# A depth of two for a stretch of input transfers in a fused DeltaNet and gated-MLP kernel

## The chip, the cores and the metric

The kernel runs on one core of one Trainium2 chip. The metric is the device time of one execution in microseconds (us). The runs of the kernel before lie at 631.19, 631.37 and 634.57 us; their median is 631.37 us.

## What is computed

```
for t in range(S):                              # _attn_ref, per batch and head
    y[:, :, t] = einsum('bhd,bhde->bhe', q[:, :, t], state)
    v_old = einsum('bhde,bhd->bhe', state, kt)  # kt: k over its norm
    state = state + bt * einsum('bhd,bhe->bhde', kt, vt - v_old)
...
gate = 1.0 / (1.0 + exp(-(x @ w_gate)))         # _moe_ref, x = y of all heads
val = x @ w_val
return (gate * val) @ w_out
```

There are 4 batches, 8 heads, 768 tokens, and a head dimension of 48. The attention output is seen as 3072 tokens of 384 features; the MLP has 1536 hidden features. All inputs and the output are float32.

## The kernel before

The 768 tokens are cut into 12 groups of 64. For each group the recurrence is solved in blocks: products of keys (`gram`, L298), a small triangular solve on VectorE (DVE) (`solve`, or `solve_halves` for the first three groups), updates of the state (`updates`, `advance`), and the rows of y (`rows`, L509). Then the group's 256 tokens (64 in each of 4 batches) pass through the MLP in 12 hidden tiles of 128: `gate_val` makes the gate and value products on TensorE (PE), L585 for group 0 and L588 later; `gated` takes the sigmoid on ScalarE (ACT), L593, and the product with the value on DVE, L594; `outp` multiplies by the output weights, L613 and L619. The gate products of two tiles alternate between two PSUM buffers, so a tile needs the product L594 of the tile two before it.

The order of the work is written out by hand; each engine executes its instructions in that order. A prologue in straight lines sets up the group 0 recurrence. From the first gate tile on, a loop over slots (`slot`, two for each hidden tile) takes the work of `plan`, `late` and `tail` for the slot, so that pieces of the next groups' recurrence and of the weight preparation stand between the MLP products.

The weights come as 36 pieces of 384 KB, numbered in the order of their use (gate, value and output weights of the hidden tiles, mixed). Each is loaded by `load_piece` (L177) as raw 64-bit words. `scaled(n)` runs two ACT instructions on piece n (L194, L196), and `join` (DVE, L208) makes the float32 weights of it. Pieces 0 to 13 are loaded by `stage` in the prologue. From piece 14 on, `scaled(n)` issues the load of piece n + 6 after its own second instruction (`EAGER, BEHIND = 14, 6`).

All input loads are issued from SyncE (SP), in the order of the program: the weight pieces, the keys (`load_k`, two halves of 192 KB, L110), the queries (`load_q`, two halves of 256 KB, L114), and the rows of keys and values (`load_rows`, 384 KB, L122, with a small load of beta, L125). An issue that has to wait holds all issues behind it on SP. The helper `pace(ins, after)` makes an instruction wait for another one; it is used to hold a load until the DVE or ACT instruction given has ended. The last part of the prologue, where the change lies, contains these loads in this order: pieces 10 and 11 and the queries of group 1, all after `state[0]["joint"]` (DVE, L437); pieces 12 and 13 after `lower_left(1)` (ACT, L370); the first part of the rows of group 1; the keys of group 2; and pieces 14 to 18, one in each `scaled(8)` to `scaled(12)`.

Around and behind these loads stand, in the prediction's steps, `advance(0)` (L531 on ACT), the solve of group 1 with its transposition L429 on DVE and its products `pz` and `pm` (L416) on PE, and the solve's last subtraction L437.

Of the kernel before, what the change touches and what calls it, by code (L numbers as in the profile page):

```python
# [23 lines left out]
B, H, S, D = 4, 8, 768, 48  # L24
# [7 lines left out]
CP = 2 * J  # L32
# [28 lines left out]
def deltanet_gated_mlp(ctx: ExitStack, tc: tile.TileContext, kd, qd, kv, beta, words, out):  # L61
    nc = tc.nc
# [12 lines left out]
    kqp = [const.tile([128, 6, J, C], F32, name=f"kqp{i}") for i in range(2)]  # L75
# [15 lines left out]
    def pace(ins, after):  # L91
        if after is not None:
            tc.add_manual_dep(ins.ins, after.ins.name, mybir.DependencyInfo(mybir.DependencyClass.Sync, mybir.DependencyReason.DATA), reason="pace")
# [7 lines left out]
    def busy_array(out, n, after=()):  # L101

        for i in range(n):
            ins = nc.tensor.matmul(out=out.rearrange("q a b -> q (a b)"), lhsT=flat[:, 0:128], rhs=flat, start=True, stop=True)
            if i < len(after):
                pace(ins, after[i])

    def load_k(g):
        for e in range(2):
            nc.sync.dma_start(kqp[g % 2][64 * e:64 * e + D, 0:2].rearrange("p s c t -> p (s c t)"), kd[g, e])  # L110

    def load_q(g, after=None):
        for e in range(2):
            ins = nc.sync.dma_start(kqp[g % 2][64 * e:64 * e + 64, 2 + 2 * e:4 + 2 * e].rearrange("p s c t -> p (s c t)"), qd[g, e])  # L114
            pace(ins, after)

    def load_rows(g, part):

        st = state[g]
        if "kv" not in st:  # L120
            st["kv"] = wk.tile([128, 2, CP, D], F32, name=f"kv_{g}", tag="kv", bufs=2)
        nc.sync.dma_start(st["kv"][:, part].rearrange("p c d -> p (c d)"), kv[g, :, part * CP * D:(part + 1) * CP * D])  # L122
        if part:
            st["beta"] = wk.tile([128, 32], F32, name=f"beta_{g}", tag="beta", bufs=2)
            nc.sync.dma_start(st["beta"], beta[:, g])  # L125

    def load_group(g):
        load_k(g)
        load_q(g)
        load_rows(g, 1)  # L130
        load_rows(g, 0)
# [42 lines left out]
    def load_piece(n, after=None):  # L174
        f, w = pieces[n]
        raw[n] = wt.tile([128, PW, 2], U32, name=f"raw_{n}", tag=f"w{n}")
        ins = nc.sync.dma_start(raw[n].rearrange("p c w -> p (c w)"), words[3 * f + "gvo".index(w)])  # L177
        pace(ins, after)

    def stage(lo, hi, after=None):  # L180
        for n in range(lo, hi):
            load_piece(n, after)
# [6 lines left out]
    def scaled(n):  # L189

        half, lo, hi = words_of(n)
        nc.scalar.activation(lo.bitcast(I32), half, AF.Copy, bias=-4095.5 / 8192, scale=1 / 8192)  # L194
        h = hi.bitcast(F32)
        done[n] = nc.scalar.activation(h, h, AF.Prelu, scale=2.0 ** -112, alpha=-2.0 ** 32)  # L196
        if n + BEHIND in range(EAGER, len(pieces)):
            load_piece(n + BEHIND, done[n])
# [336 lines left out]
    def flip(g, c):  # L535

        st = state[g]
        if c == 0:
            xx = wk.tile([128, 2, KC, GT], F32R if g else F32, name=f"xx_{g}", tag=f"xx{(g + 1) % 2}", bufs=1)
            st["xh"], st["xl"] = (xx[:, i] for i in range(2))  # L540
        xh, xl, ys = st["xh"], st["xl"], st["ys"][:, c].rearrange("p h e d -> p (h e d)")
        pt = ps_aux.tile([128, KC, 128], F32, name=f"pt_{g}_{c}", tag="aux")
        for k in range(KC):
            nc.tensor.transpose(pt[:, k], ys[:, k * 128:(k + 1) * 128], ident)
        ts = slice(c * 128, (c + 1) * 128)
        if g == 0:
            (nc.vector.tensor_copy if c else nc.scalar.copy)(out=xh[:, :, ts], in_=pt)  # L547
            return
        nc.scalar.copy(xh[:, :, ts], pt)
        nc.vector.tensor_tensor(out=xl[:, :, ts], in0=pt, in1=xh[:, :, ts].bitcast(F32), op=ALU.subtract)  # L550
# [103 lines left out]
    def take(gen, n=1):  # L654
        for _ in range(n):
            next(gen, None)
# [11 lines left out]
    EN = mybir.EngineType  # L668
    ctx.enter_context(tc.manual_schedule(engines={EN.DVE, EN.PE, EN.Activation, EN.Pool, EN.SP}))
    load_k(0)  # L670
    load_rows(0, 1)
    load_q(0)
    stage(0, 3)
    load_k(1)
    stage(3, 6)
    load_rows(0, 0)
# [20 lines left out]
        scaled(n)  # L697
    take(norms1, 11)
    take(halves0, 2)
    stage(10, 12, state[0]["joint"])  # L700
    load_q(1, state[0]["joint"])
    clear(1)
    take(masks0, 2)
# [22 lines left out]
    flip(0, 0)  # L726
    flip(0, 1)
    busy_array(gap[0], 2)
    tail = collections.defaultdict(list)
    for n, at in enumerate((0, 0, 1, 2, 3, 5, 6, 8, 9, 10, 10, 11, 11, 12, 12, 13, 14, 15, 16, 16, 17, 18, 18), 13):  # L730
        plan[at].append(lambda n=n: scaled(n))
# [153 lines left out]
```

## Time and profile before

| | |
|---|---|
| median of 3 runs | 631.37 us (631.19 to 634.57) |
| profiled execution, its own time | 631.45 us |
| span of the profiled execution | 629.7 us |
| PE busy | 610.1 us, 97% of the span |
| DVE busy | 478.4 us, 76% |
| ACT busy | 345.1 us, 55% |
| PE clock granted | 1.00 |
| hardware DMA queue q1 | 17664 packets, 39.53 MB |
| weight pieces | 36 issues of 384 KB, median 6.0 us to landing |

The span runs from the first to the last instruction of the program; the execution's own time has what lies around it too. All times in the profile are counted from the span's start. A timeline row gives start, length, engine, line, operation, what is written and read, the count of merged instructions, and in brackets the idle time of the engine before it and what ended it. A row of a DMA issue gives the count, the size and the median time from the issue to the landing. Names such as L177 are line numbers of the kernel before. SPq rows are issues of transfers by SP. The chain that ended last is followed back from the last instruction, each step to what released it.

### The profile page before, as it was taken

To read this page: it belongs to the slowest core of one execution; us is meant where nothing else is said; L and a number is where in the kernel's file an instruction comes from. 1 tells how busy PE (TensorE), PEld (TensorE's weight loads), DVE (VectorE), ACT (ScalarE), POOL (GpSimd) and SP (SyncE) were. 2 spreads that over 40 slices of the span, in tenths; PEclk is the share of its full clock that TensorE was granted. 3 is DMA by queue.
4 is the path that set the end of the run, shared out by engine and by line. 5 is a ranking of instruction groups with operands and counts; after the bars stand their busy time and mean duration, and the time that the engine had idled before them with its cause. 6 is when DMAs were issued, how large, how long until landed. Compare 5 with 4: busy or idle time off the path is not lost.

```text
span 629.7 us, 25087 instructions
## 1 busy us (share of the span) xinstructions
PE 610.1 (97%) x10990; PEld 566.3 (90%) x10998; DVE 478.4 (76%) x1443; ACT 345.1 (55%) x933; POOL 40.7 (6%) x102
## 2 busy tenths in 40 slices
PE   6789999999999999999999999999999999999996
PEld 3467778899999999999999999999999999999996
DVE  5887887688978978978977977977977977963221
ACT  4889775477446446456456456456456456435222
POOL 6000000000002002002001002002002002001000
PEclk9999999999999999999999999999999999999999
DMA  8495742203113113113113103112113100100101
GB/s 260 179 303 186 248 108 70 55 2 87 28 27 87 27 28 87 28 28 86 28 29 87 27 28 88 26 29 86 28 29 86 26 4 4 26 4 2 26 1 25
DMA packets 17773, 41.13 MB, mean 65 GB/s; under 512 B 4224, under 2 KB 7296, under 8 KB 17664
## 3 DMA queue, kind: packets, MB, share of 16 engines
q1 hardware_dynamic: 17664, 39.53, 22.5%
q8 instruction: 86, 1.41, 0.9%
q14 instruction: 23, 0.19, 0.1%
HBM read 34.80 MB, written 4.72 MB: 63 GB/s over the span
## 4 chain that ended last, share of the span: by engine, by line
PE 89%; DVE 7%; issue 1%; ACT 1%; DMA 1%; ACTq 0%; SPq 0%; DVEq 0%
PE gv L588 44%; PE po L619 21%; PE gv L585 5%; PE pu L488 3%; PE po L613 3%; PE yy L509 2%; PE pg L298 2%; PE pp L326 2%; PE pk L457 2%; PE pd L527 1%; PE pk L480 1%; DVE w L224 1%; PE pm L416 1%; DMA kqp<-in_kd_dram 1%; DVE hg L402 1%
## 5 line engine op out<-in xcount | busy, mean ns | idle before, releaser
L588 PE MATMUL gv<-xx,w 128*128 128x256 f32 x2376 | 311.6, 285 | 0.3 <-DVE xx L550 0.3
L588 PEld LDWEIGHTS gv<-xx,w 128*128 128x128 f32 x2376 | 299.0, 191 | 4.0 <-DVE xx L550 0.6
L619 PE MATMUL po<-w,h 128*128 128x384 f32 x792 | 162.7, 341 | 0.0
L619 PEld LDWEIGHTS po<-w,h 128*128 128x128 f32 x792 | 133.7, 188 | 1.2
L599 ACT CAST h<-sg 128x256 fp32r<-128x256 f32 x132 | 53.5, 405 | 116.0 <-DVE sg L594 115.7
L593 ACT ACTIVATE sg<-gv 128x256 f32<-128x256 f32 x144 | 54.9, 381 | 110.8 <-PE gv L588 103.4
L594 DVE TENSOR_TENSOR sg<-sg,gv 128x256 f32<-128x256 f32 x144 | 60.1, 417 | 66.2 <-ACT sg L593 65.9
L354 DVE TENSOR_TENSOR tmp<-X,gp 128x126 f32<-128x126 f32 (+22 forms) x279 | 73.4, 263 | 8.2
L357 DVE TENSOR_TENSOR X<-X,tmp 128x126 f32<-128x126 f32 (+22 forms) x279 | 72.3, 259 | 8.3
L604 DVE TENSOR_TENSOR h<-sg,h 128x256 fp32r<-128x256 f32 x132 | 54.9, 416 | 12.5 <-ACT h L599 12.4
L564 POOL COPY x<-yt 32x192 f32<-32x192 f32 x72 | 29.4, 409 | 444.6 <-DVE yt L559 441.9
L491 ACT COPY su<-pu 32x384 f32<-32x384 f32 x92 | 43.3, 470 | 10.9 <-PE pu L488 9.1
L284 ACT ACTIVATE kv<-kv,mq 128x48 f32<-128x48 f32 x192 | 47.9, 325 | 0.0
L331 DVE TENSOR_TENSOR kqp<-pp,pmask 64x512 f32<-64x512 f32 x48 | 33.0, 688 | 1.5 <-PE pp L326 0.2
L585 PE MATMUL gv<-xx,u 128*128 128x256 f32 x144 | 33.6, 384 | 0.3 <-DVE xx L547 0.3
L585 PEld LDWEIGHTS gv<-xx,u 128*128 128x128 f32 x144 | 26.7, 190 | 5.1 <-ACT xx L547 0.8
L468 DVE TENSOR_TENSOR R<-kv,pk 128x384 f32<-128x384 f32 x44 | 22.4, 550 | 10.1 <-PE pk L480 9.3
L310 ACT COPY G<-pg 32x256 f32<-32x256 f32 (+1 forms) x69 | 25.4, 368 | 8.0 <-PE pg L298 6.6
L564 ACT COPY x<-yt 32x192 f32<-32x192 f32 x72 | 25.1, 349 | 1.2
L559 DVE STREAM_TRANSPOSE yt<-ys 128x768 f32<-128x768 f32 x9 | 8.8, 979 | 19.9 <-ACT ys L515 19.9
L217 ACT CAST w<-u 128x384 fp32r<-128x384 f32 x36 | 18.0, 507 | 9.3 <-DVE w L224 9.2
L533 DVE TENSOR_TENSOR su<-su,pd 48x384 f32<-48x384 f32 x40 | 22.0, 550 | 0.5
(107 smaller groups left out, 543.6 us busy)
## 6 DMA issues: line engine op xcount, KB each, us to landing
raw<-in_words_dram SPq DMA_DIRECT2D x36, 384.0 KB, 6.0
kv<-in_kv_dram SPq DMA_DIRECT2D x24, 384.0 KB, 3.8
kqp<-in_qd_dram SPq DMA_DIRECT2D x24, 256.0 KB, 4.3
kqp<-in_kd_dram SPq DMA_DIRECT2D x24, 192.0 KB, 3.5
out_dram<-ot SPq DMA_DIRECT2D x48, 96.0 KB, 2.2
beta<-in_beta_dram SPq DMA_DIRECT2D x12, 16.0 KB, 3.5
```

The costliest lines, as they stand in the source:

```text
L284: nc.scalar.activation(V[:, c], V[:, c], AF.Copy, scale=mq[:, c, 0:1])
L354: nc.vector.tensor_tensor(out=tmp, in0=X[:, k:16, j:j + 1].to_broadcast([128, n, j]), in1=gp[:, j:j + 1, 0:j].to_broadcast([128, n, j]), o ...
L357: nc.vector.tensor_tensor(out=X[:, k:16, 0:j], in0=X[:, k:16, 0:j], in1=tmp, op=ALU.add)
L491: (nc.vector.tensor_copy if g == 0 and x else nc.scalar.copy)(out=su[r:r + 32, 2 * x + e], in_=pu[x][r:r + 32])
L564: copy(x[32 * q:32 * q + 32, :, :, a].rearrange("q k c s -> q c k s"), yt[32 * a:32 * a + 32, :, q::4])
L585: nc.tensor.matmul(out=pg[:, o], lhsT=parts[w, f][:, k * 128:(k + 1) * 128], rhs=x[0][:, k], start=k == 0, stop=k == KC - 1)
L588: nc.tensor.matmul(out=pg[:, o], lhsT=parts[w, f][:, a, k * 128:(k + 1) * 128], rhs=x[b][:, k], start=(k == 0 and q == 0), stop=(k == KC - ...
L593: nc.scalar.activation(h, st["gv", f][:, 0], AF.Sigmoid)
L594: nc.vector.tensor_tensor(out=h, in0=h, in1=st["gv", f][:, 1], op=ALU.mult)
L599: nc.scalar.copy(hh[:, 0], st["sg", f])
L604: nc.vector.tensor_tensor(out=hh[:, 1], in0=st["sg", f], in1=hh[:, 0].bitcast(F32), op=ALU.subtract)
L619: nc.tensor.matmul(out=po[s], lhsT=hh[:, a, ts], rhs=parts["o", f][:, w], start=(f == 0 and q == 0), stop=(f == NF - 1 and q == 2))
```

## The change

Every load of keys, queries, rows and weight pieces is noted in a list `sent` as it is issued (the loads of beta are not). While a depth stands in `behind`, each noted load waits, besides what it waited for already, until the load that many positions before it in the list has landed. The depth is 2; it is set just before pieces 10 and 11 are issued, the eleventh and twelfth, and taken away just before the first slot, in which the first gate tile is.

```
+    sent, behind = [], []
+
+    def in_turn(ins):
+
+        if behind and len(sent) >= behind[0]:
+            pace(ins, sent[-behind[0]])
+        sent.append(ins)
+
     def load_k(g):
         for e in range(2):
-            nc.sync.dma_start(...)
+            in_turn(nc.sync.dma_start(...))
...
     def load_q(g, after=None):
...
             pace(ins, after)
+            in_turn(ins)
...
     def load_rows(g, part):
...
-        nc.sync.dma_start(st["kv"][:, part]...)
+        in_turn(nc.sync.dma_start(st["kv"][:, part]...))
...
     def load_piece(n, after=None):
...
         pace(ins, after)
+        in_turn(ins)
...
     take(halves0, 2)
+    behind.append(2)
     stage(10, 12, state[0]["joint"])
     load_q(1, state[0]["joint"])
...
     busy_array(gap[0], 2)
+    behind.clear()
     tail = collections.defaultdict(list)
```

More of the change, by code (lines that the diff above doesn't have):

```diff
@@ L106, in busy_array, with in_turn @@
                 pace(ins, after[i])
+    sent, behind = [], []
+    def in_turn(ins):
+        if behind and len(sent) >= behind[0]:
+            pace(ins, sent[-behind[0]])
+        sent.append(ins)
     def load_k(g):
         for e in range(2):
-            nc.sync.dma_start(kqp[g % 2][64 * e:64 * e + D, 0:2].rearrange("p s c t -> p (s c t)"), kd[g, e])
+            in_turn(nc.sync.dma_start(kqp[g % 2][64 * e:64 * e + D, 0:2].rearrange("p s c t -> p (s c t)"), kd[g, e]))
     def load_q(g, after=None):
@@ L115, in load_q @@
             pace(ins, after)
+            in_turn(ins)
     def load_rows(g, part):
@@ L121, in load_rows @@
             st["kv"] = wk.tile([128, 2, CP, D], F32, name=f"kv_{g}", tag="kv", bufs=2)
-        nc.sync.dma_start(st["kv"][:, part].rearrange("p c d -> p (c d)"), kv[g, :, part * CP * D:(part + 1) * CP * D])
+        in_turn(nc.sync.dma_start(st["kv"][:, part].rearrange("p c d -> p (c d)"), kv[g, :, part * CP * D:(part + 1) * CP * D]))
         if part:
@@ L178, in load_piece @@
         pace(ins, after)
+        in_turn(ins)
     def stage(lo, hi, after=None):
@@ L699, in deltanet_gated_mlp @@
     take(halves0, 2)
+    behind.append(2)
     stage(10, 12, state[0]["joint"])
@@ L728, in deltanet_gated_mlp @@
     busy_array(gap[0], 2)
+    behind.clear()
     tail = collections.defaultdict(list)
```

## The prediction

> **What bounds the kernel now.** I read the page first, then the chain of work that ended last, then the timelines of SP, ACT, DVE and PE one by one over 28 to 72 us, where the changed transfers lie.
>
> ```profile
> span 629.7 us, 25087 instructions
> PE 89%; DVE 7%; issue 1%; ACT 1%; DMA 1%; ACTq 0%; SPq 0%; DVEq 0%
> ...
> 42.45 5.42 PE L585 MATMUL gv<-xx,u 128*128 128x256 f32 x24 [0.31 <-DVE xx L547]
> 47.80 1.16 PE L298 MATMUL pg<-kqp 48*64 48x64 f32 x64
> ```
>
> The whole kernel is a PE stream: 89% of the chain is PE. From the first gate tile at 42.45 us (the rows with start, length, engine, line and what is written) PE is fed almost without a break, so whatever stops it there for a moment is added to the end. Loads matter only where they make somebody late for PE. These are the loads concerned, on SP's queue (start, length of the issues, line, count), and the DVE instruction that releases the first:
>
> ```profile
> 28.27 0.69 DVE L437 TENSOR_TENSOR mt<-mt,pm 128x512 f32<-128x512 f32 x1 [0.44 <-PE pm L416]
> ...
> 28.98 1.29 SPq L177 DMA_DIRECT2D raw<-in_words_dram  x2
> 30.32 1.11 SPq L114 DMA_DIRECT2D kqp<-in_qd_dram  x2
> 33.22 0.81 SPq L177 DMA_DIRECT2D raw<-in_words_dram  x2
> 34.08 1.27 SPq L122 DMA_DIRECT2D kv<-in_kv_dram  x1
> 35.45 0.88 SPq L110 DMA_DIRECT2D kqp<-in_kd_dram  x2
> 36.42 11.41 SPq L177 DMA_DIRECT2D raw<-in_words_dram  x9
> ```
>
> In program order these are pieces 10, 11, both halves of q(1), pieces 12, 13, rows kv(1) part 0, both halves of k(2), then pieces 14, 15, 16, 17, 18 as their scaling slots come. That is fourteen paced transfers; the last four raw issues of the last row (19 and on) are not paced. Up to eight are in flight at a time, they crowd each other, and each takes long:
>
> ```profile
> raw<-in_words_dram SPq DMA_DIRECT2D x9, 384.0 KB, 6.0
> kqp<-in_kd_dram SPq DMA_DIRECT2D x2, 192.0 KB, 7.0
> ```
>
> (transfers issued from 28.9 to 43 us: count, size, median us from issue to landing). What ACT does with the pieces, one pair L194/L196 for each, piece 12 first:
>
> ```profile
> 40.88 0.56 ACT L194 ACTIVATE raw<-raw 128x384 int32<-128x384 uint16 x1
> 42.14 0.56 ACT L194 ACTIVATE raw<-raw 128x384 int32<-128x384 uint16 x1
> 43.98 0.55 ACT L194 ACTIVATE raw<-raw 128x384 int32<-128x384 uint16 x1 [0.84 <-DMA raw<-in_words_dram]
> 45.59 0.56 ACT L194 ACTIVATE raw<-raw 128x384 int32<-128x384 uint16 x1
> 48.19 0.56 ACT L194 ACTIVATE raw<-raw 128x384 int32<-128x384 uint16 x1
> 48.65 0.56 ACT L196 ACTIVATE raw<-raw 128x384 f32<-128x384 f32 x1
> 49.74 1.93 ACT L531 COPY su<-pd 48x384 f32<-48x384 f32 x4 [0.53 <-PE pd L527]
> 59.52 0.38 ACT L593 ACTIVATE sg<-gv 128x256 f32<-128x256 f32 x1
> ```
>
> The L194 rows are pieces 12, 13, 14, 15 and 17. Only piece 14 is waited for, for 0.84 us; so there is no margin for piece 14 already before the change, and little for the next ones. From 49.74 to 59.52 ACT has no idle time that could take up a delay (next row: stretch, its length, then busy us of PE, PEld, DVE, ACT: 5.85 of 6.00).
>
> ```profile
> 54.00:60.00 6.00, 6.00 (x27) 4.75 (x26) 2.88 (x10) 5.85 (x18) 0.53 (x1) 1.00 0.38 97
> 60.00:66.00 6.00, 5.29 (x282) 4.03 (x281) 5.86 (x15) 4.77 (x16) 0.00 (x0) 1.00 0.64 205
> ```
>
> **The change part by part.** Nothing is removed. It adds bookkeeping at build time, which costs nothing on the chip, and one more wait before each of the fourteen issues. SP executes its queue in order, so each wait also holds everything behind it on SP, and at most two of the fourteen are in flight. Of the fourteen, the first two wait for pieces 8 and 9, which landed long before (SP had stood idle until L437 ended at 28.96), so they keep their start. After that two chains run side by side, each transfer starting when the one two ahead has landed:
> even: piece 10, q(1) first half, piece 12, kv(1), k(2) second half, piece 15, piece 17;
> odd: piece 11, q(1) second half, piece 13, k(2) first half, piece 14, piece 16, piece 18.
>
> The restart after a landing I take as 0.05 us: SP started 0.02 us after L437 ended, and a second wait instruction may stand between. The price of a transfer with one other beside it is the term that decides. It was not run in this form, so it is bounded by rows from quieter stretches:
>
> ```profile
> raw<-in_words_dram SPq DMA_DIRECT2D x1, 384.0 KB, 3.1
> raw<-in_words_dram SPq DMA_DIRECT2D x5, 384.0 KB, 3.5
> raw<-in_words_dram SPq DMA_DIRECT2D x1, 384.0 KB, 3.7
> kv<-in_kv_dram SPq DMA_DIRECT2D x1, 384.0 KB, 3.2
> kv<-in_kv_dram SPq DMA_DIRECT2D x1, 384.0 KB, 3.9
> kqp<-in_qd_dram SPq DMA_DIRECT2D x1, 256.0 KB, 3.6
> kqp<-in_qd_dram SPq DMA_DIRECT2D x1, 256.0 KB, 4.5
> kqp<-in_kd_dram SPq DMA_DIRECT2D x1, 192.0 KB, 2.9
> kqp<-in_kd_dram SPq DMA_DIRECT2D x16, 192.0 KB, 3.3
> ```
>
> The 3.1 is piece 10 itself (issued at 28.98), the 3.5 the median of the five pieces issued from 63 to 72 us, with one or two in flight, the 3.7 a piece issued just behind another, at 67.8 us. The others are from the later loads of a group, which come two to four close together; 3.3 is the median of all later k loads. I take 3.4 for a piece (nearest to the 63 to 72 us stretch, a little less because its last one had three beside it), 3.4 for kv, 3.1 for k, and 3.7 for q (near its low end: its rows are of two halves issued close together, the paced ones will start at the landings of pieces 10 and 11, about 1 us apart).
>
> Even chain: piece 10 lands at 28.98 + 3.1 = 32.1. Then 3.7 + 3.4 + 3.4 + 3.1 + 3.4 + 3.4 = 20.4, with six restarts 0.3, is 20.7: piece 17 lands at 52.8. Low ends: 3.6 + 3.1 + 3.2 + 2.9 + 3.1 + 3.1 + 0.3 = 19.3, at 51.4. High ends: 4.5 + 3.7 + 3.9 + 3.3 + 3.7 + 3.7 + 0.3 = 23.1, at 55.2.
> On the way piece 12 lands at 39.3 (high 40.4), needed at 40.88; k(2) at 45.9 (high 47.7), needed by PE's L298 at 47.80; piece 15 at 49.3 instead of in time for 45.59.
> Odd chain: piece 11 goes 0.4 us behind piece 10 and lands, as the second of a pair (3.7), at 33.1. Piece 13 lands at 40.3 (high 41.4), needed at 42.14: no cost. Piece 14: 3.7 + 3.4 + 3.1 + 3.4 + 0.2 = 13.8, at 46.9 instead of 43.98.
>
> So ACT stands three times: for piece 14 until 46.9, for piece 15 until 49.3, and for piece 17 until 52.8. The waits don't add; each piece is due at an absolute time and the last one decides. The pair for piece 17 takes 48.65 + 0.56 - 48.19 = 1.02 us, so L531, which began at 49.74, begins at about 53.85: ACT is 4.1 us late. It stays 4.1 late to the sigmoid of 59.52 (63.6), as it has no gap between.
>
> Behind that sigmoid stands DVE, and behind DVE stands PE:
>
> ```profile
> 59.93 0.42 DVE L594 TENSOR_TENSOR sg<-sg,gv 128x256 f32<-128x256 f32 x1 [2.94 <-ACT sg L593]
> 66.09 0.70 DVE L429 STREAM_TRANSPOSE scratch<-mt 128x512 f32<-128x512 f32 x1
> 65.24 2.86 PE L585 MATMUL gv<-xx,u 128*128 128x256 f32 x12
> 68.03 0.72 PE L416 MATMUL pm<-scratch 32*32 32x32 f32 x60
> 69.06 0.79 PE L416 MATMUL pm<-scratch 32*32 32x32 f32 x68 [0.31 <-issue]
> ```
>
> DVE's L594 waits for exactly this sigmoid and from it DVE is full (5.86 of 6.00 us from 60 to 66), so L429, which ended at 66.79, ends at 70.9. The products pm read what L429 writes; PE came to them at 68.1 (65.24 + 2.86), 1.3 us after L429, and so could hide 1.3 of the 4.1 us. Now it comes to them at 68.1 and starts at 70.95: 2.85 us lost. Smaller stops of PE before that, for a gate buffer that the late sigmoid frees, are swallowed by this wait. Some 0.2 us may come back, as the 0.31 us in which PE waited for nothing the profile shows, in the middle of pm, can pass while it waits anyway. After pm PE goes on in its order with the delay, and DVE and ACT, later still by up to 1.3 us, have idle time to come back to it:
>
> ```profile
> 74.38 0.42 DVE L594 TENSOR_TENSOR sg<-sg,gv 128x256 f32<-128x256 f32 x1 [1.22 <-ACT sg L593]
> ```
>
> Nothing later is tied to an absolute time, so the rest moves as a block: +2.65 us.
>
> The profiled execution took 631.45 us (its span 629.7 and 1.75 around it), 0.08 over the median 631.37. 631.45 + 2.65 = 634.1. Low prices: L531 at 52.45, 2.7 late, minus 1.3 and 0.3, is +1.1, 632.6. High prices: L531 at 56.25, 6.5 late, minus 1.3, is +5.2, 636.7.
>
> **The rivals.** About 0.5%, 3.16 us here, is what a measurement of this kernel can tell from no change.
>
> *The chain is dearer (slower).* If piece 17 lands after about 53.3, 0.5 us later than I take, the loss passes 3.16 us. That is 0.08 us more per transfer, and q alone at its high end gives 0.8. For it: the high rows above, and that an issue itself took up to 1.27 us (kv at 34.08). Against: with two in flight most crowding is gone. With the middle of its stretch at 54.2 L531 is at 55.25, 5.5 late, the loss 4.1: 635.5.
>
> *The waits are hidden (no change).* If piece 17 lands by 50.0, L531 is at most 1.3 us late and the slack before pm takes it. That needs 17.9 us for six transfers, 2.93 each with the restart; only the lowest k row is that short. Time 631.4.
> [...]
>
> *Not slower, a shade faster.* PE waits twice for nothing that the profile shows while the crowd is in flight:
>
> ```profile
> 31.18 0.28 PE L488 MATMUL pu<-kv,mt 32*32 32x48 f32 x5 [1.31 <-issue]
> 36.56 0.37 PE L488 MATMUL pu<-kv,mt 32*32 32x48 f32 x14 [0.67 <-issue]
> ```
>
> Both lie on the chain before the first gate tile. If the crowd of loads causes the second (the first begins before anything paced differs), a thinner one takes up to 0.67 us away and PE starts the gates earlier. It counts only if piece 17 is in time too, by 50.0; else ACT, which waits for landings, sets the pace anyhow. Time 630.8.
>
> *The change doesn't do what it says.* If the added edge between two issues of one queue made no wait, nothing would change, 631.4. Against it: a wait of the same kind, pace on the instruction given, held SP until 28.98 here.
>
> **How the numbers follow.** Forecast as summed, landing of piece 17 between 50.8 and 53.3 (632.3 to 634.6): 0.50. Dearer chain: 0.38. Hidden: 0.07. Shade faster: 0.03. No wait made: 0.02. Over 0.5% slower is the dearer chain, 0.38; over 0.5% faster only by a cause I don't see, 0.02, taken from the rest; within 0.5% all else, 0.60. The range reaches from just under the low sum into the hidden case, 632.0, to 636.5 near the high sum, leaving 1 in 10 on each side.
>
> **What would show it.** SP's raw issues of the stretch spread from 28.98 to about 50, each soon after a landing, with 3.1 to 3.7 us to landing instead of 6.0; ACT's waits on raw landings rise from 0.84 to some 6 us (3.8 for piece 14, over 1 each for 15 and 17); L531 starts near 53.8; PE shows a wait of 2 to 3 us on DVE's L429 before pm, and later the same idle times as now. It is wrong if piece 17 lands before 50, if PE stops at another place first for longer, or if the delay shrinks again after 75 us.

## The result and the profile after

The changed kernel took 635.83 us (median of 6 runs, 632.97 to 636.26) against 631.08 us (6 runs) before: a ratio of 1.006, 95% interval 1.0032 to 1.0088 (the two medians alone would give 1.0075). It is slower by a little over half a per cent. The execution that was profiled was the quickest of the six, 632.97 us with a span of 631.3, so its trace shows only 1.5 us of the loss; a second profile of the same kernel, further down, shows the rest.

Transfers issued from 28.5 to 49 us in the changed kernel (count, size, median us to landing):

```profile
raw<-in_words_dram SPq DMA_DIRECT2D x7, 384.0 KB, 3.6
kqp<-in_qd_dram SPq DMA_DIRECT2D x2, 256.0 KB, 3.4
kv<-in_kv_dram SPq DMA_DIRECT2D x1, 384.0 KB, 3.2
kqp<-in_kd_dram SPq DMA_DIRECT2D x2, 192.0 KB, 3.1
```

SP's timeline of the same kernel (start, length, what is issued):

```profile
28.61 0.95 SPq L186 DMA_DIRECT2D raw<-in_words_dram  x2
31.78 1.68 SPq L122 DMA_DIRECT2D kqp<-in_qd_dram  x2
35.30 1.18 SPq L186 DMA_DIRECT2D raw<-in_words_dram  x2
```

The median transfer takes 3.1 to 3.6 us, where it took 6.0 (pieces) and 7.0 (keys) before, but each one starts only when the one two ahead of it has landed, so that they come in pairs. ACT's timeline (in brackets the idle time and what ended it; L204/L206 are L194/L196 of before, L541 is L531, L603 is the sigmoid):

```profile
48.18 0.55 ACT L204 ACTIVATE raw<-raw 128x384 int32<-128x384 uint16 x1 [6.43 <-DMA raw<-in_words_dram]
51.10 0.57 ACT L204 ACTIVATE raw<-raw 128x384 int32<-128x384 uint16 x1 [0.79 <-DMA raw<-in_words_dram]
52.81 0.56 ACT L204 ACTIVATE raw<-raw 128x384 int32<-128x384 uint16 x1 [0.41 <-DMA raw<-in_words_dram]
53.71 0.45 ACT L541 COPY su<-pd 48x384 f32<-48x384 f32 x1
```

Those are the waits for pieces 14, 16 and 17. What DVE makes of it, from its timeline:

```profile
63.92 0.42 DVE L604 TENSOR_TENSOR sg<-sg,gv 128x256 f32<-128x256 f32 x1 [2.98 <-ACT sg L603]
70.09 0.70 DVE L439 STREAM_TRANSPOSE scratch<-mt 128x512 f32<-128x512 f32 x1
```

And PE:

```profile
49.94 1.35 PE L595 MATMUL gv<-xx,u 128*128 128x256 f32 x5 [1.31 <-DVE sg L604]
70.94 1.28 PE L426 MATMUL pm<-scratch 32*32 32x32 f32 x128 [2.27 <-DVE scratch L439]
73.54 2.75 PE L595 MATMUL gv<-xx,u 128*128 128x256 f32 x12
```

PE stops twice, 1.31 us before gate tile 2 and 2.27 us before pm. The chain of work that ended last now runs through the loads themselves, one behind the other, up to the late scaling (start, length, what):

```profile
29.04 3.68 DMA raw<-in_words_dram
32.78 3.35 DMA kqp<-in_qd_dram
36.14 3.62 DMA raw<-in_words_dram
39.82 3.20 DMA kqp<-in_kd_dram
43.08 5.07 DMA raw<-in_words_dram
...
49.19 3.59 DMA raw<-in_words_dram
...
70.09 0.71 DVE scratch L439
```

The first five DMA rows are the odd chain of the prediction, from piece 11 to piece 14; the last is piece 17 of the even chain, issued when piece 15 had landed.

### The profile page after: what moved, and what is told of

It is laid out like the page before. It is cut to its first block, busy times and chain, and to the rows that moved or that the text cites. A ratio compares the mean times of both kernels' runs of the same rounds, so it can differ in the third digit from the quotient of the medians.

```text
span 631.3 us, 25085 instructions
## 1 busy us (share of the span) xinstructions
PE 610.0 (97%) x10990; PEld 565.9 (90%) x10998; DVE 478.4 (76%) x1443; ACT 344.7 (55%) x933; POOL 40.7 (6%) x102
## 4 chain that ended last, share of the span: by engine, by line
PE 84%; DVE 7%; DMA 4%; ACT 3%; issue 1%; SPq 0%; ACTq 0%; DVEq 0%
PE gv L598 44%; PE po L629 21%; PE gv L595 3%; PE pu L498 3%; DMA raw<-in_words_dram 3%; PE yy L519 2%; PE po L623 2%; PE pg L308 2%; PE pp L336 2%; PE pk L467 1%; PE pk L490 1%; PE pd L537 1%; DMA kqp<-in_kd_dram 1%; DVE w L234 1%; ACT kv L294 1%
## 5 line engine op out<-in xcount | busy, mean ns | idle before, releaser
L609 ACT CAST h<-sg 128x256 fp32r<-128x256 f32 x132 | 53.5, 405 | 116.2 <-DVE sg L604 115.8
L603 ACT ACTIVATE sg<-gv 128x256 f32<-128x256 f32 x144 | 54.9, 381 | 109.6 <-PE gv L598 103.0
L204 ACT ACTIVATE raw<-raw 128x384 int32<-128x384 uint16 x36 | 20.2, 561 | 8.0 <-DMA raw<-in_words_dram 7.9
```

Of the source, the lines that this page charges most:

```text
L603: nc.scalar.activation(h, st["gv", f][:, 0], AF.Sigmoid)
L609: nc.scalar.copy(hh[:, 0], st["sg", f])
```

## The experiments

Each was timed on the same chip as the kernel before, side by side with it. That kernel's median was 631.17 on the first chip (r1 to r4), 631.60 on the second (r5 to r8) and 632.91 on the third (r9 to r12); so ratios are compared, not times across chips. Theory A is the prediction's: due times, piece 17 and the transposition before pm. B is the PE clock, C a cost of every wait, D a delay that moves on to the next place.

| run | median us | ratio, 95% interval |
|---|---|---|
| r1 changed kernel again | 636.24 | 1.008 (1.0056 to 1.0104) |
| r2 depth 4 | 631.57 | 1.0005 (0.999 to 1.0019) |
| r3 depth 1 | 652.50 | 1.034 (1.031 to 1.0369) |
| r4 matmuls in the stop | 637.23 | 1.0092 (1.0064 to 1.012) |
| r5 pm a tile later | 638.09 | 1.0105 (1.0068 to 1.0141) |
| r6 the same, piece 14 later | 636.59 | 1.0081 (1.0058 to 1.0104) |
| r7 needed loads first, depth 2 | 633.08 | 1.0015 (0.9996 to 1.0034) |
| r8 needed loads first, free | 631.13 | 0.9981 (0.9965 to 0.9997) |
| r9 transposition early | 634.78 | 1.0032 (1.0007 to 1.0057) |
| r10 back half only | 632.89 | 1.0006 (0.9984 to 1.0028) |
| r11 front half only | 631.86 | 0.9986 (0.9968 to 1.0005) |
| r12 as r8 | 631.32 | 0.9977 (0.9957 to 0.9997) |

**The changed kernel once more** (no edit).

> The changed kernel once more, for the spread of its times and the granted clock in each. Theory A (late piece): the time is set by when piece 17 lands; in the first profile it landed at 52.78 us, PE stood 2.27 us before pm, and the whole was 1.5 us longer than before. By A the runs near 636 us are runs in which piece 17 lands later, some 55 to 56 us, with a granted clock like that of the others. Theory B (clock): the runs near 636 us are runs in which the stop of PE before pm lowers the granted clock for a few us afterwards; by B the piece lands at 52 to 53 us in them too, the mean clock is 0.996 against 0.999, and this is worth about 0.003 x 634 = 1.9 us. Both expect a median of 634 to 636.5.

Measured: 635.34 to 637.2. Its profiled execution took 635.64, so it shows the common case. ACT's timeline at piece 17:

```profile
53.79 0.58 ACT L204 ACTIVATE raw<-raw 128x384 int32<-128x384 uint16 x1 [0.79 <-DMA raw<-in_words_dram]
```

PE's timeline behind it:

```profile
71.95 1.70 PE L426 MATMUL pm<-scratch 32*32 32x32 f32 x128 [2.26 <-DVE scratch L439]
73.58 2.65 PE L623 MATMUL po<-u,sg 128*128 128x384 f32 x4
```

Two stretches of 3.41 us (busy us of PE, PEld, DVE, ACT, POOL, then the granted clock, DMA share, GB/s):

```profile
69.00:72.41 3.41, 1.15 (x58) 0.75 (x58) 3.27 (x11) 3.41 (x10) 0.00 (x0) 1.00 0.79 238
72.41:75.82 3.41, 3.41 (x99) 2.44 (x89) 3.24 (x12) 3.17 (x8) 0.00 (x0) 0.50 0.91 305
```

Both theories have a part, and neither has its number. Piece 17 came 1.0 us later than in the first profile (53.8 against 52.8, where A said 55 to 56 and B 52 to 53), and behind the stop the granted clock was 0.50 for 3.41 us (and 1.00 again from 75.82 to 79.24). With it pm took 1.70 us instead of 1.28 and the four po products 2.65, where the kernel before has 1.56 (L613 at 69.78 in its timeline); together 1.5 us. In the first profile the two stretches of 3.41 us that hold the same stop both kept the full clock, and so did the next, to 76.75 (the same columns):

```profile
66.51:69.92 3.41, 2.17 (x11) 1.56 (x9) 3.31 (x10) 3.41 (x10) 0.00 (x0) 1.00 0.52 153
69.92:73.34 3.42, 2.40 (x132) 1.99 (x133) 3.28 (x12) 3.42 (x10) 0.00 (x0) 1.00 0.88 263
```

Nor does B's other number hold: a run's mean clock doesn't tell its time (637.2 us at 0.990, but 635.34 at 0.991 and 636.89 at 0.997); so what a half clock costs would have to differ with its place, which no run here isolates. How many of the unprofiled runs had it behind pm is not known.

**The depth** (r2, r3): `behind.append(2)` becomes 4, or 1.

> Depth 4 instead of 2. Theory A: with four in flight a transfer has about twice the time; piece 14 is issued at about 39.8, when piece 13 lands, and lands at 44 to 44.5; piece 17 is issued at 43.2 and lands at 47.5 to 48.5, before 50.0, so L531 is on time, PE does not stop before pm, and the time is that of the kernel before, 630.0 to 631.5 us. Theory C (each added wait costs by itself, in SP or in the landing, whatever the depth): 14 waits as in the changed kernel, so 633 to 636 us.

> Depth 1: each of the transfers waits for the one just ahead. Theory A by the measured times of a transfer alone (piece 3.15, q 3.4, kv 3.2, k 3.05, each with 0.05): piece 12 lands at 45.0 (due 40.9), piece 14 at about 61, piece 17 at about 70.3; L531 begins at 71.3 and is 21.6 us late, pm comes to 88 instead of 68: about 20 us longer, 651 us (648 to 654), and PE stands in several places of which the longest is over 10 us. Theory B adds to that a granted clock clearly below 0.99 because of the long stops. Theory C: about as the changed kernel, 633 to 637 us.

Depth 4 is the kernel before in time (ratio 1.0005), with the same fourteen waits: at this depth the waits as such cost nothing that shows, and C is out for it. Piece 14 landed at 42.9 and piece 17 at 47.5, and ACT waits for no piece (it took piece 14 at 44.58 and piece 17 at 50.08). At depth 1, piece 12 landed at 45.5, piece 14 at 61.7 and piece 17 at 70.75 (expected 45.0, about 61, 70.3), and the time is 21.3 us longer (expected about 20). Its PE stops, with their waits in brackets:

```profile
46.91 6.92 PE L595 MATMUL gv<-xx,u 128*128 128x256 f32 x24 [5.49 <-ACT xx L557]
58.58 1.87 PE L308 MATMUL pg<-kqp 48*64 48x64 f32 x59 [3.56 <-DMA kqp<-in_kd_dram]
75.94 4.27 PE L595 MATMUL gv<-xx,u 128*128 128x256 f32 x12 [2.18 <-DVE sg L604]
```

The sum is right, but I expected one stop of over 10 us, and it is several up to 5.5. The granted clock was 0.50 from 43.1 to 49.9 and from 56.75 to 66.98, around the stops of 5.49, 3.56 and 1.57 us, and behind the one of 2.18 it was 0.81 from 75.13 to 78.55 and 0.69 from 78.55 to 81.96. pm came at 89.0 (expected 88).

**Work in the stop** (r4).

```
+        if g == 1:
+            busy_array(pm, 8)
         blocks(pm, D, Z)
```

> The changed kernel with eight more matmuls on the constant mask (as the prologue has them) into pm before its products for group 1, so that PE works for about 1.9 us in the stop before pm, whose result is overwritten. Theory A: the stop shrinks from 2.3 to about 0.4 us of idle time, but pm starts when L429 ends, at about 70.9, as before: the same time as the changed kernel, 634 to 636.5 us median, with the same spread. Theory B: the clock is not lowered any more, no run shows 0.996, and the runs near 636 us are gone: median 633 us (632.5 to 634).

It doesn't support B: 637.23, no better than r1. But it was no clean test. In its trace piece 17 came only at 55.3, the granted clock was 0.50 at two other places, from 60.76 to 64.17 behind a stop of 1.92 us before gate tile 4 and from 71.00 to 74.41 behind one of 1.62 us inside pz, and the stop at pm wasn't there to be filled. ACT's timelines at piece 17, here (r4) and in the next run (r5):

```profile
55.28 0.56 ACT L204 ACTIVATE raw<-raw 128x384 int32<-128x384 uint16 x1 [2.56 <-DMA raw<-in_words_dram]
55.50 0.57 ACT L204 ACTIVATE raw<-raw 128x384 int32<-128x384 uint16 x1 [2.11 <-DMA raw<-in_words_dram]
```

**pm later in PE's order** (r5, r6).

```
-    late[10].append(steps(halves1))
+    late[12].append(steps(halves1))
```

With it the subtraction L447 moves from `plan[11]` to `plan[13]`; in r6 also the scaling of piece 14 from slot 0 to slot 1.

> The changed kernel with the products pm of group 1 one gate tile later in PE's order (behind gate tile 6, before the subtraction that needs them, which also goes one tile later). Loads and their waits are unchanged. Theory A (PE stops at pm because piece 17 is late, and nowhere else for long): the stop of 2.3 us before pm and the half clock that follows it are gone, what is left are the 1.3 to 1.5 us before gate tile 2, less what the thinner loads give in the prologue (first gate tile 1 us earlier): 631 to 632.5 us, clock as before. Theory D (the delay is in ACT and DVE and comes out at the next place anyway): PE stops for about as long before the update products behind gate tile 6 or at a gate buffer: 634.5 to 636.5 us.

> As the one before, and the scaling of piece 14 behind the first sigmoid in ACT's order instead of ahead of it, so that the wait for piece 14 doesn't hold the sigmoid that frees gate tile 2's buffer. Theory A: the stop before gate tile 2 (1.3 to 1.5 us) goes too, and with the first gate tile 1 us earlier the whole is 630 to 631 us, by 0 to 1 us below the kernel before, though every load still waits at depth 2. Theory D: 634 to 636.5 us.

Both went D's way, and beyond its ranges. The stop moved behind gate tile 6, to the products that need L447, and grew (r5):

```profile
80.95 1.50 PE L498 MATMUL pu<-R,mt 32*32 32x48 f32 x64 [3.16 <-DVE mt L447]
```

My edit is part of this: it put L447 two slots back on a DVE that was late and full (busy for 3.31 of the 3.41 us from 76.93). Another part isn't: piece 17 came at 55.5 in this trace, 1.7 us later than in r1, though its load is issued as there. What the run can show is that the delay is carried by DVE's order, not where it must come out. In r6 the stop before gate tile 2 went, and 1.28 us before gate tile 3 came instead.

**The transposition early** (r9): loads untouched, one DVE instruction moved (L439 of the changed kernel, to behind L418).

```
         nc.vector.transpose(mt..., X...)
+        if g == 1:
+            nc.vector.transpose(D..., mt...)
         yield
...
-        nc.vector.transpose(D..., mt...)
+        if g != 1:
+            nc.vector.transpose(D..., mt...)
```

> The changed kernel, loads and waits as they are, with one DVE instruction moved: the transposition for pm (L439 of the changed kernel) directly behind the transposition it reads (L418), into the 3 us in which DVE waits for the late sigmoid. Theory A (PE stops before pm because this transposition stands behind DVE's full stretch, which is late by piece 17): pm starts at 68.7 instead of 70.9 to 71.9, the stop of 2.3 us is gone and no half clock follows it; the update products behind gate tile 6 find their operand ready at 73.7. Time 632 to 634 us, 2.5 to 4 us under the changed kernel; what is left is the stop before gate tile 2. Theory D (the delay comes out at the next place): PE stops before the update products or at a gate buffer for about 2 us, 635 to 637 us.

This is the clean form of the question. DVE does it in its idle time, PE hardly stops before pm, and the products behind gate tile 6 find their operand:

```profile
61.66 0.71 DVE L420 STREAM_TRANSPOSE scratch<-mt 128x512 f32<-128x512 f32 x1
...
69.33 1.29 PE L428 MATMUL pm<-scratch 32*32 32x32 f32 x128 [0.51 <-ACT scratch L443]
75.92 0.88 PE L501 MATMUL pu<-R,mt 32*32 32x48 f32 x64
```

The profiled execution is the quickest of twelve (632.10 us, the median is 634.78), so what the common run has more is not seen. The excess over the kernel before falls from 5.1 us (r1) to 1.9, though piece 17 landed at 53.5. So the wait for L439, and what follows it, is some 3 us of the 5 (give or take 2, by the two intervals); the rest has the stop before gate tile 2, still 1.10 us here. The median in us is above the 632 to 634 expected, on a chip where the kernel before is 1.7 us above its time on r1's chip; the saving is in the range.

**Half of the waits** (r10, r11): the depth is set only before `load_k(2)`, or taken away there.

> Depth 2 only from the keys of group 2 on (those and pieces 14 to 18); pieces 10 to 13, the queries and the rows of group 1 are free. Theory A: the chain starts from the crowded landings of piece 13 (39.7) and the rows (41.4), and by 3.1 to 3.4 a step piece 17 lands at 50.5 to 51.5, 1 to 2 us earlier than in the changed kernel: L541 is 2 to 2.5 us late, PE stops 1 us before pm, which rarely lowers the clock: 632 to 633.5 us.

> Depth 2 only for pieces 10 to 13, the queries and the rows of group 1; the keys of group 2 and pieces 14 to 18 are free. Theory A: the free ones are issued at 39 to 42 and land at 44 (piece 14) to 48 (piece 17), in time; PE has no stop before gate tile 2 or pm; with the thinner prologue the first gate tile is at about 41.5: 629.5 to 631 us, at or a little below the kernel before. Theory C (each added wait costs): 632 to 634 us.

With the back half alone piece 17 landed at 50.7, PE had no stop before pm (which began at 71.0 for other reasons, below), and the time is that of before. As PE came late to pm by itself, this run doesn't show whether the loss begins at 50.0, the prediction's slack. With the front half alone piece 17 landed at 48.9 and the time is not above before, though ACT waited 4.1 us for piece 14, until 45.9. So a piece 14 that was 2 us later than in the kernel before, with piece 17 in time, cost PE no stop. Neither half costs by itself.

**The order instead of the depth** (r7, r8, r12): queries and rows of group 1 behind piece 18; depth 2 in r7, none in r8 and r12.

```
     stage(10, 12, state[0]["joint"])
-    load_q(1, state[0]["joint"])
...
     stage(12, 14, lower_left(1))
-    load_rows(1, 0)
...
+    load_q(1)
+    load_rows(1, 0)
     behind.clear()
     tail = collections.defaultdict(list)
```

> Depth 2 as in the changed kernel, but the queries and the first rows of group 1, which are not needed before 75 us, are issued behind piece 18. Theory A (it is the due times, not the depth): piece 14 lands at 43 to 44, piece 15 at 43.5 to 45, piece 17 at 47 to 48.5; ACT hardly waits, PE doesn't stop before gate tile 2 or pm, and with the prologue 1 us shorter the time is 629.5 to 631 us, at or a little below the kernel before. Theory C (depth 2 costs by itself): 634 us or more.

> The same order of loads with no depth at all. Theory A, with the prologue's gain put down to the thinner loads: pieces land a little earlier still, the first gate tile is at about 42.4 as in the kernel before (the 0.67 us in which PE waited for nothing the profile shows near 36 us come back), so 630.5 to 631.5 us, up to 1 us above the run at depth 2. If the prologue's gain has nothing to do with the depth, both are alike within 0.3 us.

> The free order with the queries and rows of group 1 behind piece 18, once more. If its 0.2% under the kernel before is real, the ratio is again 0.997 to 0.9995; if not, the interval holds 1 with a median at or above it.

At depth 2 the pieces came when they were expected to (piece 14 at 42.4, piece 17 at 48.3), ACT waits for one only (0.39 us for piece 17), and 3.6 us of r1's 5.1 are gone. But 633.08 lies between what A and C gave, and is not below the kernel before. PE's timeline of r7 has a stop for which the profile names no releaser:

```profile
65.45 0.68 PE L426 MATMUL pz<-mt,scratch 32*32 32x32 f32 x56 [1.91 <-issue]
```

The two stretches around it, columns as above:

```profile
63.33:66.74 3.41, 1.50 (x83) 1.29 (x70) 3.27 (x11) 0.98 (x4) 0.00 (x0) 1.00 0.71 226
66.74:70.15 3.41, 3.41 (x10) 2.70 (x9) 1.32 (x6) 1.79 (x5) 0.00 (x0) 0.50 0.38 121
```

The kernel before stops there too, for 0.71 us. Free of the depth, the same order (r8) is 1.9 us quicker than r7 on the same chip by the means, 630.97 against 632.85. So depth 2 seems to cost something even where the pieces are in time; whether this stop is how, and why it is longer, no run isolates. The free order is the fastest kernel of the study, by 0.2% on two chips, each interval just below 1. That is better than both kernels, and small. My reason for its gain was wrong in part: I expected the first gate tile at 42.4 without the depth, and it came at 41.64, about as with it (42.06).

## Why the prediction was right, and where it was short

The time fell into the range, 632.0 to 636.5, and the place and the path were as forecast. In the first profile piece 17 was to land at 52.8 and ACT took it at 52.81; L531 was to begin at 53.85 and began at 53.71; pm was to start at 70.95 and started at 70.94. ACT's waits were to be some 6 us and were 7.6. r9 and r2 show that this path, and not the waits as such, is most of the loss; r7 against r8 leaves some 2 us that it doesn't explain. That the numbers agree so closely is luck, as the first two points below say, and that profile is of the quickest run. And the likeliest outcome was missed: I gave 0.60 to a change within 0.5% and 0.38 to slower, and both measurements of the changed kernel are above 0.5%.

Point by point:

- *The price of a transfer* (q 3.7, piece 3.4, kv 3.4, k 3.1): q 3.4, kv 3.2, k 3.1 and a median piece 3.6 in the first profile. There the errors cancel: the chain began 0.4 us earlier, q, kv and k took 0.5 us less, and pieces 12, 15 and 17 took 0.8 more. In the five other profiles with the loads of the changed kernel piece 17 landed later, at 53.5 (r9), 53.8 (r1), 54.1 (r6), 55.3 (r4) and 55.5 (r5). All are past the 53.3 of the rival "the chain is dearer", and two past the high end of 55.2. So the term for a piece was too low, by up to 2.3 us (piece 17 in r4 took 5.7), and the dearer chain is what five of the six profiles show; its 635.5 us is nearer to the medians of 635.83 and 636.24 than the 634.1 of the sum. How dear a piece is beside one other was worked out from quieter stretches; why it varies (2.8 to 5.7 us) stays open. The crowd before was a little overstated too: by issue and landing, at most seven transfers were in flight before, not eight.
- *Piece 14* was to land at 46.9, and took 5.1 us instead of 3.4, so ACT took it at 48.18. This term was too small. That the smaller stop for a gate buffer is swallowed by the one before pm did hold: the stop before gate tile 2 was 1.31 us (1.52 in r1), it changes nothing as long as L439 is later still, and it comes to the surface in r9. Why piece 14 was slow (4.4 to 5.1 us in the six profiles with these loads) stays open.
- *The gain in the prologue*, up to 0.67 us, stood as a rival of its own with 0.03. It came in full, together with the loss: the first gate tile began at 41.39 against 42.45 (0.37 us of it because L437 had ended earlier), and the wait of 0.67 us at 36.56 was gone. As I had said for that case, it didn't count, since ACT waits for landings.
- *"Nothing later is tied to an absolute time, so the rest moves as a block"* failed in two ways. One gives time back, which I had named as a sign of being wrong ("if the delay shrinks again after 75 us"): from gate tile 6 (73.54 against 71.17, 2.4 us behind) to the end the first profile recovers 0.85 us at group 2's pz and pm, where in the kernel before PE waited 0.43 us for nothing that the profile shows. PE's timeline of before:

```profile
116.18 0.67 PE L416 MATMUL pz<-mt,scratch 32*32 32x32 f32 x54 [0.27 <-issue]
119.96 0.82 PE L416 MATMUL pm<-scratch 32*32 32x32 f32 x73 [0.16 <-issue]
```

And of the changed kernel:

```profile
117.46 1.28 PE L426 MATMUL pz<-mt,scratch 32*32 32x32 f32 x128 [0.41 <-DVE kqp L341]
121.01 1.29 PE L426 MATMUL pm<-scratch 32*32 32x32 f32 x128
```

- The other takes time, and is the term the sum lacked: *the clock behind a stop*. In r1 it was 1.5 us. Forecast 2.65, later piece 1.0 and half clock 1.5 make 5.15; gate tile 6 began 4.90 us later in r1 than before (76.07 against 71.17), and with 0.75 recovered at group 2's products the span is 4.2 us longer (633.9 against 629.7). The sum was made from rows of before, where the granted clock was 1.00 from 28 us to PE's last product, and I had no term for what a forecast stop of 2 to 3 us might do to it.

## What to carry to other kernels

A depth on a queue of loads turns each landing time into a sum of latencies (here 3.68, 3.35, 3.62, 3.20 and 5.07 us up to piece 14); add them up along the chain and compare each with the moment its user is due, since here most of the loss came from the one load that was late for longest. Take the prices from rows of the same kind, and give the sum a spread as wide as theirs. When many loads crowd each other, try first to put those that are due last at the end: here this gained 0.2%, where the depth cost 0.6 to 0.8%. When a forecast has a stop of the array, add as a possible term what half the clock behind it would cost: here stops of 1.42 (r10) to 2.26 us (r1) were followed by 3.4 us at 0.50, and one of 2.27 us (first profile) was not.

## What was not expected of the hardware

The granted clock was halved behind some short stops of PE and not behind others as long. In stretches of 3.4 us at 1.00, PE was busy for 0.86 (r5), 1.15 (r1), 1.50 (r4 and r7), 1.79 (r4) and 2.00 us (r10) where the stretch behind had 0.50, and for 1.86 (before, from 28.39 to 31.80), 2.17 and 2.40 us (first profile) where it had 1.00. So PE's busy time in such a stretch doesn't by itself tell the two apart. The stop of 2.26 us before pm in r1 cost 1.5 us more through the clock, the one of 2.27 us in the first profile nothing; what decides between them no run isolates.

PE's stops for which no releaser is named are as large as what the whole change was about. The one near 36 us was 0.67 us before and 1.50 in r2 and r10, the three traces in which four loads are in flight by 30.9 us. It is absent in all others, where at most two are until 33 us. PE's timeline of r10:

```profile
37.16 0.37 PE L498 MATMUL pu<-kv,mt 32*32 32x48 f32 x14 [1.50 <-issue]
```

And of r8, where the same products run through:

```profile
34.77 0.88 PE L498 MATMUL pu<-kv,mt 32*32 32x48 f32 x62 [0.20 <-DVE kv L478]
```

Another stands inside pz near 64 to 70 us: 0.71 before, 0.16 in r9, 1.42 in r10, 1.62 in r4 and 1.91 in r7. It doesn't follow the depth, and the three long ones were each followed by a granted clock of 0.50 for 3.4 us (r10 from 67.02, r4 from 71.00, r7 from 66.74). In r10 the gate products ahead of pm, from 66.55, took 4.54 us (2.86 before), which is why pm was late there. A stop of 1.61 us inside pz of r3, up to 85.65, was followed by 1.00. In the trace of before a transfer of 16 KB on the instruction queue (q8) began at 34.01 us, 2.55 us before PE went on at 36.56, and another at 61.81, 2.82 us before it went on at 64.63; in the first profile one began at 62.46, 2.76 us before PE went on at 65.22, and one at 35.90 behind which PE ran through. Whether these transfers have to do with the stops no run here tested.
